# Warm-up matmuls of TensorE in 32x32 tiles of 512 columns, in place of 128x128

## The chip, the cores and the metric

The kernel runs on one core of a Trainium2 chip. The metric is the device time of one execution in microseconds (us). The kernel before the change takes 1802.02 us (median of 3 runs, 1801.92 to 1802.12).

## The reference

The reference mixes two blocks over the same 2048 tokens of 1024 features, with a gate per token. Cut to what matters:

```python
def _A_ref(x, wqkv, wo):                       # attention, 32 heads of 32
    qkv = (x @ wqkv) ...                       # (1024 x 3072) projection
    scores = einsum("bhqd,bhkd->bhqk", q, k) * Dh ** -0.5
    p = softmax(scores); o = einsum("bhqk,bhkd->bhqd", p, v)
    return o @ wo
def _B_ref(x, w_q, k1, k2, u, v):              # 32 routers, each picks 1 of 64 experts
    q = einsum("nd,dhc->nhc", x, w_q); s1 = q1 . k1; s2 = q2 . k2
    e = argmax(s1) * 8 + argmax(s2)
    return sum over h of gelu(x . u[e]) * v[e]
g = sigmoid((x * gate_w).sum(-1, keepdims=True))
return g * a + (1 - g) * b
```

Nothing that the change touches enters this result: the matmuls it replaces write to PSUM banks which the projection then starts anew.

## The kernel before

One function, `gated_mha_peer_kernel`, records every instruction by hand: the schedule is manual, each engine runs its instructions in the order in which the program writes them down, and semaphores join the engines where one needs what another made. There is no planner. So the place of a statement in the source sets its place in its engine's queue, behind everything written for that engine before it.

The projection to Q and K runs in float32 by halves: `split(hi, lo, src)` (L99 to L101) has ScalarE copy `src` to a rounded half `hi` (L100) and VectorE subtract it to give the rest `lo` (L101); a product is then three matmuls (hi.hi, hi.lo, lo.hi). The tokens are cut in four blocks of 512 columns, the 1024 features in eight chunks of 128 (`kc`).

The change lies in the first 30 us of the program, which run as follows.

- Constants: VectorE writes `ones` and an identity matrix `ident` of 128x128 (L96, from an iota of GpSimd).
- Loads of the first weights (`wraw`, by the queues of ScalarE and SyncE) and of the tokens (`xh`, `xl` places, by SyncE) are issued chunk by chunk.
- Splits of the first chunk are written down before any matmul: `split_w0(0, 1)` for the weights of chunk 0, `split_x(0)` for its tokens (two blocks), and then already `split_w0(1, 2)`, the weights of chunk 1. Their halves go to tiles `e` and `xh`.
- Four PSUM banks `b0` are taken (banks 0 to 3), and the warm-up matmuls follow: nine times `ident` by `ident` into the last of the banks (L391). They read nothing but `ident`.
- `mm0` (L395) is the first real product: weights of Q and K chunk 0, two token blocks, eight chunks `kc`, three matmuls each: 96 matmuls of 512 columns into the four banks. The first of each bank starts the bank anew (`start=True`). The splits of chunks 1 to 7 are written between them, chunk by chunk.
- The next product is a plain loop over the same tokens (L491), with the router's folds (`fold`, L311: four matmuls of 32 output columns each, one per quarter of the array) in between. Then come six rounds of a Strassen product (`product`, L155), plain chunks again (L711), the routers (L758, L926), V (L155), attention (`ring` L1292, `o` L1313) and the output projection (`pa`).

The tile pool `ev` with three buffers a name holds the tiles `hi` and `lo` in which the results of the projection are put (`evac_hi`, L240, and `evac_lo`, L253).

The lines around the change:

```python
    split_w0(0, 1)
    split_x(0)
    load_w0(4, KC, nc.sync)
    dma(kraw, k12.rearrange("p (a e) -> p a e", a=2))
    split_w0(1, 2)
...
    b0 = {(w, n): bank() for w in range(2) for n in (2, 3)}
    for i in range(9):                                                             # L390
        nc.tensor.matmul(b0[1, 3][:, :128], ident, ident, start=True, stop=True)   # L391
    def mm0(w, n, kc, i):
        a, b = ((0, 0), (0, 1), (1, 0))[i]
        nc.tensor.matmul(b0[w, n], w_parts[w, kc // HC][:, a, kc % HC], x_at(b, n, kc),
                         start=(kc == 0 and i == 0), stop=(kc == KC - 1 and i == 2))
```

Of the kernel before, what the change touches and what calls it, by code (L numbers as in the profile page):

```python
# [10 lines left out]
F32 = mybir.dt.float32  # L11
# [21 lines left out]
def gated_mha_peer_kernel(ctx, tc, xT, wqkv, wv, wo, wq, k12, ug, v, out):  # L33
# [8 lines left out]
    nc = tc.nc  # L42
# [22 lines left out]
    ident = const.tile([128, 128], F32, name="ident")  # L65
# [128 lines left out]
    def bank():  # L194
        while bank_no[0] % 8 in held:
            bank_no[0] += 1
        i = bank_no[0] % 8
        bank_no[0] += 1
        return ps1.tile([128, 512], F32, name=f"bk{i}")
# [6 lines left out]
    ev = Pool("ev", bufs=3)  # L206
# [180 lines left out]
    b0 = {(w, n): bank() for w in range(2) for n in (2, 3)}  # L387


    for i in range(9):  # L390
        nc.tensor.matmul(b0[1, 3][:, :128], ident, ident, start=True, stop=True)  # L391

    def mm0(w, n, kc, i):
        a, b = ((0, 0), (0, 1), (1, 0))[i]
# [90 lines left out]
    for w in range(2):  # L485
        for n in (2, 3):
            ps = bank()
# [216 lines left out]
    for blk, (k, n) in enumerate(order):  # L704
        w, c = chunks[k]
        t = pairs[k % 2]
        ps = bank()
# [1126 lines left out]
```

## Time and profile before

| | before |
|---|---|
| median of 3 runs | 1802.02 us |
| profiled execution, its own time | 1801.88 us |
| span of its instructions | 1800.1 us |
| TensorE busy (PE) | 1793.7 us, 100% |
| VectorE (DVE), ScalarE (ACT) | 1502.7 us (83%), 1216.7 us (68%) |
| first warm-up matmul, first `mm0` matmul, first L491 matmul | 1.52, 6.14, 30.23 us |

A busy share is the share of the span in which an engine had an instruction under way. PE is the matmul side of TensorE, PEld its weight loads, which overlap. A matmul's record runs longer than its slot, as matmuls are pipelined: the distance from one start to the next is what it costs. A float32 matmul leaves two records, so the nine of the warm-up show as 18, and the four of a fold as 8; a matmul on halves (fp32r) leaves one. The PEclk of the profile is the clock that a throttle granted; it is 1.00 throughout.

### The profile page before, as it was taken

The numbers are of one execution on the slowest core, as the hardware profiler recorded it, in microseconds if no ns is written. First come the engines' busy times: TensorE is split into PE (matmuls) and PEld (weight loads), VectorE is DVE, ScalarE is ACT, GpSimd is POOL, SyncE is SP. The second block draws the span as 40 slices with busy tenths as digits, with TensorE's granted clock in tenths as the row PEclk, the third lists the DMA queues.
The fourth block names the chain that finished last, engine by engine and source line by source line (L and its number), as shares of the span: only waits on it lengthen the run. The fifth ranks groups of instructions, "written<-read, shape, count | busy, mean of one in ns | idle before, by whom it ended". The sixth has DMA issues, their size and how long they took to land.

```text
span 1800.1 us, 27993 instructions
## 1 busy us (share of the span) xinstructions
PE 1793.7 (100%) x10559; PEld 1135.3 (63%) x10559; DVE 1502.7 (83%) x1685; ACT 1216.7 (68%) x1604; POOL 284.0 (16%) x353
## 2 busy tenths in 40 slices
PE   9999999999999999999999999999999999999999
PEld 7877777788888845555455554555554555547887
DVE  7868776358887779899899899999989989897774
ACT  4434321211333399999999999999999999993221
POOL 0222000026401201111111121121111121222000
PEclk9999999999999999999999999999999999999999
DMA  6788889823238688899899999898999999986761
GB/s 239 240 285 252 271 265 289 270 80 107 83 115 281 231 199 176 173 188 194 181 203 200 200 197 192 190 199 190 203 211 206 203 219 190 201 176 216 233 172 59
DMA packets 130454, 359.15 MB, mean 200 GB/s; under 512 B 18648, under 2 KB 56648, under 8 KB 104764
## 3 DMA queue, kind: packets, MB, share of 16 engines
q0 software_dynamic: 22352, 132.98, 36.3%
q1 hardware_dynamic: 87804, 188.42, 36.0%
q10 hardware_dynamic: 20160, 35.92, 7.0%
q8 instruction: 84, 1.38, 0.3%
q14 instruction: 54, 0.44, 0.1%
HBM read 173.72 MB, written 86.61 MB: 145 GB/s over the span
## 4 chain that ended last, share of the span: by engine, by line
PE 98%; DMA 1%; ACT 0%; SPq 0%; issue 0%; DVE 0%; ACTq 0%; DVEq 0%
PE ring L1292 28%; PE o L1313 26%; PE bk L155 13%; PE bk L711 10%; PE pa L155 6%; PE bk L758 5%; PE pa L1571 2%; PE bk L926 2%; PE bk L311 2%; PE bk L491 1%; PE pa L1578 1%; PE bk L395 1%; DMA wraw<-in_wqkv 1%; ACT P L1301 0%; SPq L82 0%; PE o L1326 0%
## 5 line engine op out<-in xcount | busy, mean ns | idle before, releaser
L1301 ACT ACTIVATE P<-ring 128x512 f32<-128x512 f32 (+3 forms) x986 | 808.1, 942 | 14.0 <-PE ring L1292 8.6
L1353 DVE TENSOR_TENSOR acc<-acc,P 128x1024 f32<-128x1024 f32 x408 | 469.7, 1219 | 22.1 <-ACT P L1301 22.1
L1313 PE MATMUL o<-P,V 128*32 128x512 f32 (+1 forms) x4040 | 412.6, 529 | 0.0
L1292 PE MATMUL ring<-Q,K 98*128 98x512 f32 x1024 | 268.7, 406 | 0.1
L1292 PE MATMUL ring<-z,z 98*128 98x512 f32 x1020 | 267.5, 406 | 0.1
L1292 PEld LDWEIGHTS ring<-Q,K 98*128 98x128 f32 x1024 | 182.6, 188 | 116.9 <-ACT P L1301 38.8
L1292 PEld LDWEIGHTS ring<-z,z 98*128 98x128 f32 x1020 | 182.1, 188 | 114.6 <-issue 37.8
L1313 PEld LDWEIGHTS o<-P,V 128*32 128x32 f32 x4040 | 111.5, 109 | 218.3 <-issue 198.6
L1353 DVE TENSOR_TENSOR rb<-rb,P 128x1024 f32<-128x1024 f32 x186 | 214.4, 1219 | 5.6 <-ACT P L1301 5.6
L1342 POOL DMA_DIRECT2D P<-P x60 | 55.7, 928 | 354.6 <-PE o L1313 141.1
L240 ACT ACTIVATE hi<-bk 128x512 fp32r<-128x512 f32 x40 | 23.7, 595 | 117.8 <-PE bk L711 98.7
L1301 ACT ACTIVATE wo_raw<-ring 128x512 f32<-128x512 f32 (+3 forms) x115 | 97.6, 942 | 0.6
L711 PE MATMUL bk<-xh,e 128*128 128x512 f32 x384 | 94.2, 394 | 0.0
L711 PE MATMUL bk<-xl,e 128*128 128x512 f32 x384 | 92.2, 389 | 0.0
L253 DVE TENSOR_TENSOR lo<-bk,hi 128x512 fp32r<-128x512 f32 x40 | 27.6, 690 | 68.8 <-ACT hi L240 66.5
L711 PEld LDWEIGHTS bk<-xh,e 128*128 128x128 f32 x384 | 71.0, 188 | 22.0 <-issue 3.4
L711 PEld LDWEIGHTS bk<-xl,e 128*128 128x128 f32 x384 | 72.1, 188 | 15.0
L101 DVE TENSOR_TENSOR e<-wraw,e 128x512 fp32r<-128x512 f32 (+3 forms) x64 | 55.1, 868 | 27.8 <-ACT e L100 27.3
L1301 ACT ACTIVATE vhl<-ring 128x512 f32<-128x512 f32 (+3 forms) x89 | 76.9, 940 | 0.9 <-PE ring L1292 0.2
L1353 DVE TENSOR_TENSOR acc<-acc,wo_raw 128x1024 f32<-128x1024 f32 x60 | 70.2, 1219 | 1.8 <-ACT wo_raw L1301 1.8
L100 ACT ACTIVATE e<-wraw 128x512 fp32r<-128x512 f32 (+3 forms) x64 | 44.6, 705 | 36.8 <-DMA wraw<-in_wqkv 16.2
L1361 POOL DMA_DIRECT2D acc<-acc x41 | 33.7, 822 | 221.0 <-DMA acc<-acc 83.3
(308 smaller groups left out, 2494.7 us busy)
## 6 DMA issues: line engine op xcount, KB each, us to landing
P<-P POOLq DMA_DIRECT2D x60, 1024.0 KB, 10.3
wqt<-in_wq SPq DMA_DIRECT2D x26, 1024.0 KB
wraw<-in_wqkv SPq DMA_DIRECT2D x30, 512.0 KB
acc<-acc POOLq DMA_DIRECT2D x21, 512.0 KB, 6.3
qdh<-hi ACTq DMA_DIRECT2D x32, 256.0 KB
qdl<-lo ACTq DMA_DIRECT2D x32, 256.0 KB
kdh<-hi ACTq DMA_DIRECT2D x32, 256.0 KB
kdl<-lo ACTq DMA_DIRECT2D x32, 256.0 KB
```

Source lines behind the costliest of these rows:

```text
L100: nc.scalar.activation(hi, src, AF.Copy)
L101: (on or nc.vector).tensor_tensor(out=lo, in0=src, in1=hi.bitcast(F32), op=OP.subtract)
L155: nc.tensor.matmul(ps, self.a[a][i][:, k, :], self.b[b][j][k], start=(not first and k == 0 and i == j == 0), stop=(k == HC - 1 and i == 1))
L311: nc.tensor.matmul(ps[32 * quad:32 * quad + 32, :], kpad[:, quad % 2, i, :], t[:, quad, :], start=(i == 0), stop=(i == 3))
L711: nc.tensor.matmul(ps, t[:, kc // HC, a, kc % HC], x_at(b, n, kc), start=first, stop=last)
L758: nc.tensor.matmul(ps, x_at(a, t // 4, kc)[:, tok], b, start=first, stop=last)
L926: nc.tensor.matmul(p, x_at(a, t // 4, kc)[:, tok], b, start=first, stop=last)
L1292: on_ring(nc.tensor.matmul(ring[:, i, :], K[:98, kt * 128:(kt + 1) * 128], Q[:98, qc * 512:(qc + 1) * 512], start=True, stop=True), i)
L1301: on_ring(nc.scalar.activation(P[h, kt][:, q0 * 512:(q0 + m) * 512].rearrange("p (a m) -> p a m", a=m), ring[:, i:i + m, :], AF.Exp, scale ...
L1313: nc.tensor.matmul(O[h][32 * qc:32 * qc + 32, c0:c1], Vt[g][:, kt, 32 * j:32 * j + 32], p[:, qc * 512 + c0:qc * 512 + c1], start=(kt == 0) ...
L1342: nc.gpsimd.dma_start(P[h, b], P[h, a], accum_op=OP.add)
L1353: nc.vector.tensor_add(out[:, c], a[:, c], b[:, c])
```

## The change

The nine 128x128 matmuls go. In their place a tile `warm` of 128x512 is taken from the pool `ev` (the first buffer of the name `hi`), VectorE sets it to zero, and TensorE runs 32 matmuls of 32x32 stationary values by 512 columns: for each of the four column quarters `c` of the array, one on each of the four row quarters `r`, each row quarter with a bank of its own; and all sixteen twice.

```diff
-    for i in range(9):
-        nc.tensor.matmul(b0[1, 3][:, :128], ident, ident, start=True, stop=True)
+    warm = ev.tile([128, 512], F32, name="hi")
+    nc.vector.memset(warm, 0.0)
+    for i in range(2):
+        for c in range(4):
+            for r, ps in enumerate(b0.values()):
+                rows = slice(32 * r, 32 * r + 32)
+                nc.tensor.matmul(ps[32 * c:32 * c + 32, :], ident[rows, 32 * c:32 * c + 32], warm[rows, :],
+                                 start=True, stop=True)
```

The order of VectorE's queue around the new memset, as a difference of the two programs. The names `e_149` and `e_160` are the weight halves of Q and K, `xh_171` and `xh_173` the token halves of the two blocks; the first two rows are chunk 1 of the weights, the last two chunk 1 of the tokens.

```order
 L101 TENSOR_TENSOR e_149<-wraw_175,e_149 128x128
 L101 TENSOR_TENSOR e_160<-wraw_177,e_160 128x128
+L391 MEMSET hi 128x512
 L101 TENSOR_TENSOR xh_171<-xh_169,xh_171 128x512
 L101 TENSOR_TENSOR xh_173<-xh_169,xh_173 128x512
```

The memset stands behind the splits of the weights of chunk 1 and ahead of the token splits of chunk 1; nothing else on VectorE changes place.

The head of TensorE's queue before, with the engines on which a row waits (`DVE_49` is VectorE, `Activation_49` is ScalarE):

```order
L391 MATMUL bk_219<-ident 128x128 [waits DVE_49]
L391 MATMUL bk_219<-ident 128x128 x8
L395 MATMUL bk_216<-xh_171,e_149 128x512 [waits Activation_49]
L395 MATMUL bk_216<-xh_171,e_149 128x512 [waits DVE_49]
L395 MATMUL bk_216<-xh_171,e_149 128x512
```

The first row waits for `ident`; `mm0` follows the ninth warm-up matmul. The same place now, the first four of the 32 and the first row of `mm0` (now L401):

```order
L396 MATMUL bk_216<-hi,ident 32x512 [waits DVE_49]
L396 MATMUL bk_217<-hi,ident 32x512
L396 MATMUL bk_218<-hi,ident 32x512
L396 MATMUL bk_219<-hi,ident 32x512
...
L401 MATMUL bk_216<-xh_171,e_149 128x512 [waits Activation_49]
```

The first row now reads `hi`, the tile of the memset, so its wait for VectorE is a wait for the memset's place in the queue shown above; all of `mm0` stands behind the 32.

## The prediction

> **What bounds the kernel now.** I read the page first: the span, the busy times, the chain of work that ended last.
>
> ```profile
> span 1800.1 us, 27993 instructions
> PE 98%; DMA 1%; ACT 0%; SPq 0%; issue 0%; DVE 0%; ACTq 0%; DVEq 0%
> ```
>
> The chain is TensorE's own work for 98% of the span: whatever shifts that work shifts the end, unless TensorE waits somewhere later for something that does not shift with it. So I asked for the windows by stage and for TensorE's waits (engine, line waited for, total us, times, longest) of the stretch from 17.2 to 640 us.
>
> ```profile
> 0.00:30.00 30.00, 27.78 (x114) 21.79 (x114) 19.59 (x41) 16.73 (x29) 0.43 (x5) 1.00 0.78 281
> 30.00:180.00 150.00, 150.00 (x710) 115.86 (x709) 117.80 (x150) 57.09 (x89) 30.11 (x23) 1.00 0.80 249
> 380.00:480.00 100.00, 99.61 (x441) 81.63 (x440) 80.80 (x161) 12.37 (x25) 58.76 (x64) 1.00 0.19 61
> 1000.00:1590.00 590.00, 590.00 (x4121) 297.58 (x4114) 547.71 (x491) 581.56 (x731) 98.85 (x124) 1.00 0.95 199
> PE bk L758 <- ACT xu L762: 0.4, 1, 0.4
> ```
>
> The first figure behind the length of a window is PE's busy time. It is full from 30 us on, but for 0.4 us at the routers, and that one wait is for ScalarE, which itself waits there for a matmul. Only the first 30 us hold idle time, 2.2 us. That is where the change lies, so the question is when TensorE gets through the work of these 30 us. The chain there, and the timeline of the two engines:
>
> ```profile
> 17.17 13.21 PE bk L395 x57
> 30.39 5.44 PE bk L491 x24
> ...
> 0.88 0.11 DVE L72 MEMSET ones<- 128x64 f32 x1
> 1.26 0.20 DVE L96 TENSOR_SCALAR ident<-jp 128x128 f32<-128x128 int32 x1
> 1.52 4.21 PE L391 MATMUL bk<-ident 128*128 128x128 f32 x18 [1.52 <-DVE ident L96]
> 6.14 13.37 PE L395 MATMUL bk<-xh,e 128*128 128x512 f32 x48 [0.41 <-ACT xh L100]
> 9.06 0.29 DVE L101 TENSOR_TENSOR e<-wraw,e 128x128 fp32r<-128x128 f32 x1 [1.19 <-ACT e L100]
> 9.58 1.29 DVE L101 TENSOR_TENSOR xh<-xh,xh 128x512 fp32r<-128x512 f32 x2 [0.23 <-ACT xh L100]
> 13.36 0.69 DVE L101 TENSOR_TENSOR e<-wraw,e 128x512 fp32r<-128x512 f32 x1 [0.61 <-ACT e L100]
> 18.32 0.27 DVE L285 MEMSET kpad<- 128x256 f32 x1
> 19.34 11.04 PE L395 MATMUL bk<-xl,e 128*128 128x512 f32 x48
> 30.23 2.88 PE L491 MATMUL bk<-xh,e 128*128 128x512 f32 x12
> ```
>
> The warm-up fills the wait for the first data: it starts at 1.52, as soon as `ident` is there, and is over before the first `mm0` matmul can run at 6.14. The first 48 matmuls of `mm0` take 13.2 us because their chunks arrive late; the second 48 run without a stop, (30.23 - 19.34) / 48 = 0.2269 us each. Up to 17.17 the chain comes from loads and splits, after it TensorE never waits again.
>
> **The change part by part.** *The memset.* It is new on VectorE and stands behind the split of chunk 1's weights, the row at 9.06, which waits for a load by way of ScalarE. So it cannot start before 9.06 + 0.29 = 9.35. Its length by the two memset rows: 64 elements take 0.11 and 256 take 0.27, so 512 take about 0.27 + 256 x 0.16 / 192 = 0.48. It ends at 9.83. `ident` was done at 1.46 and its reader began at 1.52, a hand-over of 0.06; so the warm-up starts at **9.89**, not 1.52. Behind the memset on VectorE stand the token splits of chunk 1, which ran at 9.58 and now run about 0.25 later; all that follows is late by that much until the row at 13.36, ahead of which VectorE was idle for 0.61. So the delay is gone at 13.36. Who waits for those splits is `mm0` of chunk 1, which by the sum below does not start before 16 us: cost nothing.
>
> *The nine matmuls removed.* They ended before `mm0` could run and were hidden by the wait for data: their removal gains nothing.
>
> *The 32 matmuls added.* All of `mm0` is behind them in TensorE's queue. Their price depends on two things that the trace does not show for this form: how many 32x32 tiles run side by side, and at which clock. Rows for both:
>
> ```profile
> L391 PE MATMUL bk<-ident x18: 421/421/582, 1.5 to 5.3; 128*128 128x128 f32 x18
> L395 PE MATMUL bk<-xh,e x48: 387/393/651, 6.1 to 19.1; 128*128 128x512 f32 x48
> 89.88:90.34 0.46, 0.45 (x4) 0.16 (x8) 1.00 0.00 0
> 90.34:90.77 0.43, 0.43 (x8) 0.13 (x4) 1.00 0.00 0
> 90.77:91.20 0.43, 0.43 (x8) 0.13 (x4) 1.00 0.00 0
> 35.76 1.06 PE L311 MATMUL bk<-wqt,kpad 128*32 128x512 f32 x8
> 36.75 3.02 PE L491 MATMUL bk<-xh,e 128*128 128x512 f32 x12
> ```
>
> The three windows are a fold: four float32 matmuls of 512 columns on four column quarters start together, one new set of four records every 0.43 us (the count in a window includes the four still running). So quarters do run side by side, and the two records of a matmul are two sets. The warm-up's 18 records of 128 columns are 3.8 / 17 = 0.22 us apart, which is 0.89 for 512 columns: twice 0.43. TensorE ran at half speed there, although the granted clock reads 1.00 in both. If all sixteen tiles run side by side, the 32 matmuls are 2 x 2 = 4 sets; at half speed 4 x 0.86 to 0.89 = 3.4 to 3.6, I take **3.5**. Bounds: at full speed throughout 4 x 0.43 = 1.7; with nothing side by side 64 records in a row, 64 x 0.43 = 27.5 and more. I take four sets because the quarters of the fold behave so, with rows and columns alike separate quarters here, and half speed because TensorE has been idle before, as it had at 1.52.
>
> [...] No row here has more than four side by side.
>
> *`mm0` behind it.* Going back from 32-column tiles to the full array costs: two sets from 35.76 end at 36.62, and L491 follows at 36.75, 0.13. So `mm0` starts at 9.89 + 3.5 + 0.13 = **13.52**. Its 96 matmuls then take 96 x 0.2269 = 21.78, plus 0.14 for the restart (12 matmuls at 36.75 take 3.02, those at 30.23 take 2.88). Nothing stops it: by 13.52 the splits of chunks 0 to 2 are nearly through; the last splits of chunk 3 end at about 15.83 + 1.29 = 17.12 by the row below, and `mm0` needs them at 13.52 + 36 x 0.2269 = 21.7.
>
> ```profile
> 15.83 1.29 DVE L101 TENSOR_TENSOR xh<-xh,xh 128x512 fp32r<-128x512 f32 x2
> ```
>
> *The clock.* Before, TensorE was still slow at 5.3, 3.8 us after its warm-up began, and the 651 ns of the longest `mm0` record (its first, at 6.14, to 6.79) look slow too; then records fall to about 390. So it became fast 3.8 to 5.3 us after the start. From 9.89 that is 13.7 to 15.2: `mm0` runs slow for its first 0.2 to 1.7 us and loses half of it, 0.1 to 0.85. I take 0.5.
>
> [...]
>
> *Sum.* L491 starts at 13.52 + 21.78 + 0.14 + 0.5 = 35.94 against 30.23: **5.7 us later**. Taking `warm` from the pool of `hi` costs nothing: its readers end at 13.4, and the buffer is wanted again by the third evacuation, after 35 us. The evacuations themselves wait for `mm0` and move with it. On the profiled execution of 1801.88 (span 1800.1) the sum gives 1807.6; the median of the runs lies 0.14 above it, so I forecast **1807.7**. With its own bounds (3.4 to 3.6, and 0.1 to 0.85) the case runs from 1807.2 to 1808.2.
>
> **The rivals.** *Nine sets (15%).* Tiles run side by side only in the fours in which they are issued, and the second records of a four start together with the first of the next: 8 + 1 = 9 sets. Five at half speed (up to 4.4 us), four at full: 4.4 + 1.7 = 6.1, and `mm0` starts at 16.1, fast. L491 at 38.0, 7.8 late: 1809.8; if the clock rises late, up to 1 us more. For it: only fours are seen in the trace. [...]
>
> *Sixteen sets (8%).* Fours side by side and no overlap between fours: 5 x 0.89 + 11 x 0.43 = 9.2, `mm0` at 19.2, L491 at 41.1, 10.9 late: 1812.9. *Nothing side by side (4%).* 64 records, 5 of them slow: 4.4 + 59 x 0.43 = 29.8, 31.5 late: 1833.5.
>
> *It does not warm (8%).* The sixteen tiles run as foreseen, but small tiles do not count as work for the clock: `mm0` then runs slow for 3.8 to 5.3 us and loses 1.9 to 2.7 instead of 0.5. That is 7.1 to 7.9 late, 1809.1 to 1809.9. Against it: the tiles fill the array.
>
> *Fast from the start (4%).* The clock is up during the warm-up: 1.7 instead of 3.5, no loss behind it, 3.4 late: 1805.4. Against it the warm-up of before, slow for all its 3.8 us.
>
> *The other side: paid back at the end of attention (6%).* There the chain leaves TensorE:
>
> ```profile
> 1592.18 2.49 SPq L82
> 1596.72 3.39 DMA vhl<-vpl
> 1603.54 0.50 PE ring L1292
> ```
>
> If SyncE's loads at 1592 are held by something that does not start with TensorE, they stay where they are, and 2.49 + 3.39 = 5.9 us of waiting swallow the 5.7: 1801.9, no change, or a little faster. It decides whether the issue at 1592.18 moves with `mm0`. Against it: the step ahead of it in the chain is ScalarE's work on attention's results, which moves. For the lateness not to arise at all, `mm0` would have to start by 30.23 - 21.78 - 0.14 = 8.31, ahead of the memset's 9.35: the order excludes it.
>
> **How the numbers follow.** Forecast 55%, nine sets 15%, sixteen 8%, none 4%, no warming 8%, fast 4%, paid back 6%. About 0.2% or 3.6 us is what a measurement here can tell from no change. Slower by more: 55 + 15 + 8 + 4 + 8 = 90%; the fast case (3.4 us) and most of the paid-back one are within, 8%; faster 2%. The range goes from the fast case, 1805.4, to the sixteen sets at 1812.9; outside are the paid-back case, no overlap, and the slow half of sixteen sets, some 14%.
>
> **What would show it.** The first 32x32 row near 9.9 us and ended by VectorE's memset; its 64 records in four sets 0.86 apart, over by 13.5; the first `mm0` record at 13.5, its first few 0.43 apart and the rest 0.227 with no wait; L491 at 35.9; each later stage 5.7 later, attention's end too. A first 32x32 row near 1.6, more than four sets, or a late stage that starts at its old time makes it wrong.

## The result, and the profile after

The changed kernel takes 1807.97 us (median of 6 runs, 1807.77 to 1808.34) against 1802.07 for the kernel before beside it (6 runs): 5.9 us or 0.33% slower, ratio 1.0033, 95% interval 1.0023 to 1.0043. The forecast was 1807.7. Its profiled execution took 1808.07 us, its span is 1806.3.

The chain of work that ended last, at its head (start, length, what; all in us):

```profile
2.16 6.53 DMA wraw<-in_wqkv
8.69 0.02 issue
8.71 0.32 ACT e L100
9.03 0.02 issue
9.06 0.04 DVE e L101
9.09 0.31 issue
9.40 0.50 DVE hi L391
9.90 0.04 issue
9.94 4.08 PE bk L396 x64
14.03 22.62 PE bk L401 x96
36.65 5.44 PE bk L497 x24
```

This is the change in one view. The second load of chunk 1's weights lands at 8.7, ScalarE and VectorE split it, then VectorE runs the memset, and only then do the small matmuls start; `mm0`, the first product with data, follows them. Before, the loads reached the chain by way of the splits that `mm0` itself needed; now they reach it by way of a tile of zeros. The timeline, first rows of VectorE, then those of TensorE, answers to the one of before:

```profile
9.40 0.48 DVE L391 MEMSET hi<- 128x512 f32 x1
9.81 1.22 DVE L101 TENSOR_TENSOR xh<-xh,xh 128x512 fp32r<-128x512 f32 x2
...
14.69 1.29 DVE L101 TENSOR_TENSOR e<-wraw,e 128x512 fp32r<-128x512 f32 x2 [1.79 <-ACT e L100]
9.94 4.08 PE L396 MATMUL bk<-hi,ident 32*32 32x512 f32 x64 [9.94 <-DVE hi L391]
13.96 11.81 PE L401 MATMUL bk<-xh,e 128*128 128x512 f32 x48
25.61 11.04 PE L401 MATMUL bk<-xl,e 128*128 128x512 f32 x48
36.49 2.88 PE L497 MATMUL bk<-xh,e 128*128 128x512 f32 x12
```

L401 is L395 of before, L497 is L491: 36.49 against 30.23, 6.26 later, and the span is 6.2 longer. From 19.34 us of the old trace on, no matmul moved by more than 0.15 us against this shift. Behind its first row TensorE again waits only at the routers:

```profile
PE bk L764 <- ACT xu L768: 0.3, 1, 0.3
```

The windows of the small matmuls alone (length; PE busy and its records; weight loads and their records; granted clock; DMA share; GB/s; a count holds the records still running):

```profile
9.94:10.79 0.85, 0.85 (x16) 0.29 (x32) 1.00 0.66 215
10.79:11.64 0.85, 0.85 (x32) 0.17 (x1) 1.00 0.85 225
11.64:12.50 0.86, 0.86 (x32) 0.58 (x31) 1.00 1.13 184
12.50:13.96 1.46, 1.46 (x32) 0.00 (x0) 1.00 0.74 238
```

Sixteen records start at once, one per tile, a new set every 0.85 us: four sets, at half speed (a fold's set of 512 columns took 0.43). In the third window the weights of the second round are loaded while its matmuls should run.

### The profile page after: what moved, and what is told of

Read it like the earlier page. It is cut to its first block, busy times and chain, and to the rows that moved or that the text cites. A ratio compares the mean times of both kernels' runs of the same rounds, so it can differ in the third digit from the quotient of the medians.

```text
span 1806.3 us, 28086 instructions
## 1 busy us (share of the span) xinstructions
PE 1792.2 (99%) x10605; PEld 1132.9 (63%) x10605; DVE 1503.4 (83%) x1686; ACT 1216.9 (67%) x1604; POOL 284.0 (16%) x353
## 4 chain that ended last, share of the span: by engine, by line
PE 98%; DMA 1%; ACT 0%; SPq 0%; issue 0%; ACTq 0%; DVE 0%; DVEq 0%
PE ring L1298 28%; PE o L1319 26%; PE bk L155 13%; PE bk L717 10%; PE pa L155 6%; PE bk L764 5%; PE pa L1577 2%; PE bk L932 2%; PE bk L311 2%; PE bk L401 1%; PE bk L497 1%; PE pa L1584 1%; ACT P L1307 0%; DMA wraw<-in_wqkv 0%; DMA vhl<-vpl 0%; PE o L1332 0%
## 5 line engine op out<-in xcount | busy, mean ns | idle before, releaser
L717 PE MATMUL bk<-xh,e 128*128 128x512 f32 x384 | 94.2, 394 | 0.0
L155 PE MATMUL bk<-xh,e 128*128 128x512 f32 x288 | 68.5, 393 | 0.0
```

The costliest lines, as they stand in the source:

```text
L155: nc.tensor.matmul(ps, self.a[a][i][:, k, :], self.b[b][j][k], start=(not first and k == 0 and i == j == 0), stop=(k == HC - 1 and i == 1))
L717: nc.tensor.matmul(ps, t[:, kc // HC, a, kc % HC], x_at(b, n, kc), start=first, stop=last)
```

## The experiments

Two theories of the 5.9 us. **A, the place:** the memset stands behind work that waits for loads, the warm-up waits for the memset, and `mm0` for the warm-up; the form of the matmuls is harmless. **B, the form:** the small tiles cost, by their length, by the change back to the full array, or by not raising the clock. All edits are to the changed kernel.

**The memset early.**

```diff
+    warm = ev.tile([128, 512], F32, name="hi")
+    nc.vector.memset(warm, 0.0)
     split_w0(0, 1)
...
-    warm = ev.tile([128, 512], F32, name="hi")
-    nc.vector.memset(warm, 0.0)
     for i in range(2):
```

> The memset is written ahead of the first splits, so it is the first thing on VectorE after the identity; the 32 small matmuls stay as they are. Theory A (the place of the memset in VectorE's queue holds the warm-up, and all of the projection behind it): memset from 1.5 to 1.9 us, small matmuls 2.0 to 6.0, first real matmul at 6.1 to 6.3, L491's counterpart at 30.2 to 30.6, median 1801.9 to 1802.5. Theory B (the small-tile form itself costs, by its length, its mode change or a clock it does not raise): most of the 5.9 us stays, median 1804.5 or more.

Measured: 1801.64 us against 1801.78 before, ratio 1.0000 (0.9991 to 1.0009). The timeline:

```profile
1.52 0.48 DVE L376 MEMSET hi<- 128x512 f32 x1
2.06 4.09 PE L396 MATMUL bk<-hi,ident 32*32 32x512 f32 x64 [2.06 <-DVE hi L376]
6.25 12.75 PE L401 MATMUL bk<-xh,e 128*128 128x512 f32 x48
29.71 2.88 PE L497 MATMUL bk<-xh,e 128*128 128x512 f32 x12
```

The same 32 matmuls, as long as in the changed kernel, now fit into the wait for the first data. The whole loss is gone; theory B cannot say that.

**The memset on another engine.**

```diff
-    nc.vector.memset(warm, 0.0)
+    nc.gpsimd.memset(warm, 0.0)
```

> The memset stays where it is written but goes to GpSimd, whose queue holds only the iota ahead of it. Theory A: it ends by about 2 us, the small matmuls run from 2 to 6.1, and the median is that of the kernel before within 0.5 us: 1801.7 to 1802.6. Theory B: as for the early memset, 1804.5 or more.

Measured: 1801.79, ratio 0.9999 (0.9990 to 1.0008). One word, at the place in the source where the change has it: GpSimd's queue is empty behind the iota, and the row reads

```profile
1.04 0.52 POOL L391 MEMSET hi<- 128x512 f32 x1
```

so the memset was over at 1.56, and the small matmuls started at 1.78, when `ident` (over at 1.63) was there too. It was the queue, not the statement.

**The old matmuls, late.**

```diff
-    for i in range(2):
-        ...
+    for i in range(9):
+        nc.tensor.matmul(b0[1, 3][:, :128], ident, warm[:, :128], start=True, stop=True)
```

> The nine matmuls of 128x128 by 128 columns of before, but with the zeroed tile as moving operand, so that they wait for the memset where the change put it. Theory A: they start at 9.9, take 3.8 us at half speed, the first real matmul is at 13.9, and the median is that of the changed kernel, 1807.5 to 1808.2. Theory B (the form costs): clearly below it, 1805 or less.

Measured: 1807.66, ratio 1.0034 (1.0021 to 1.0046). The 128x128 form, made to wait for the same memset, costs the same:

```profile
9.93 4.11 PE L393 MATMUL bk<-hi,ident 128*128 128x128 f32 x18 [9.93 <-DVE hi L391]
13.79 11.15 PE L397 MATMUL bk<-xh,e 128*128 128x512 f32 x48
35.66 2.88 PE L493 MATMUL bk<-xh,e 128*128 128x512 f32 x12
```

L493 starts 5.43 late here; another 0.42 went near 123.6 us, for a cause that the trace does not name. With the two runs above, this settles it: form and place were exchanged one at a time, and the time goes with the place.

**The memset halfway,** behind the first token splits and ahead of `split_w0(1, 2)`.

```diff
     dma(kraw, k12.rearrange("p (a e) -> p a e", a=2))
+    warm = ev.tile([128, 512], F32, name="hi")
+    nc.vector.memset(warm, 0.0)
     split_w0(1, 2)
```

> The memset between the place of the first experiment and that of the change: behind the first token splits and ahead of the split of chunk 1's weights, which ended at 7.4 to 7.8 us. Theory A: the small matmuls start at 7.9 to 8.3, 1.6 to 2.0 us ahead of the changed kernel's, and the end follows one for one: median 1805.9 to 1806.4. Theory B: no change against the changed kernel, 1807.9.

Measured: 1805.78 (1805.08 to 1807.11), ratio 1.0023 (1.0014 to 1.0032), just under the range that A gave. The small matmuls started at 8.11, 1.83 ahead of the changed kernel's, and the median is 2.2 lower; against the kernel before beside each of the two, it is 4.0 late in place of 5.9, 1.9 less. In the profiled execution L497 starts at 34.94, only 1.55 ahead, since here more of `mm0` ran at half speed (below).

**No warm-up.**

```diff
-    warm = ev.tile([128, 512], F32, name="hi")
-    nc.vector.memset(warm, 0.0)
-    for i in range(2):
-        ...
```

> No warm-up at all. Theory A says that what the warm-up buys is small, because the first matmuls wait for loads anyway: the real matmuls start at 6.1 at half speed, 0.43 us apart, for 4 to 5.3 us, which loses 2 to 2.6 us of work, and the waits of before for chunks 1 and 3 (about 2 us up to 17.2) take most of it back: 0 to 0.8 us late, 1802.0 to 1802.9. Rival C (the warm-up is needed): the full loss stays, 1804.0 to 1804.7.

Measured: 1802.14 (1801.49 to 1802.66), ratio 1.0002 (0.9993 to 1.0011). Rival C is out: this kernel has next to nothing to win by a warm-up. The timeline, and what TensorE's weight loads waited for up to 30 us:

```profile
6.22 13.99 PE L393 MATMUL bk<-xh,e 128*128 128x512 f32 x48 [6.22 <-ACT xh L100]
...
PEld bk L393 <- ACT xh L100: 6.2, 1, 6.2
PEld bk L393 <- DVE xh L101: 0.4, 1, 0.4
```

After the 6.2 us up to its first data TensorE waits 0.4 us more. In the kernel before the weight loads of `mm0` waited, behind the warm-up, for the two engines that split:

```profile
PEld bk L395 <- ACT xh L100: 1.9, 5, 0.7
PEld bk L395 <- DVE xh L101: 1.3, 3, 0.4
```

The slow clock makes `mm0` late (its first 48 matmuls take 13.99 us, against 13.37 in the kernel before), and a late `mm0` finds its data ready: the loss sits where a fast clock would have waited.

**One round in place of two,** late as the change has it, run twice.

```diff
-    for i in range(2):
+    for i in range(1):
```

> The late warm-up cut to one round: 16 small matmuls in place of 32, memset where the change put it. Theory A with a clock that rises a set time after work begins (in the changed kernel about 5.2 us after 9.94): small matmuls from 9.94 to 11.7, first real matmul at 12.0, at half speed until about 15.2, so of the 2.0 us won about 1.0 is lost again: median 1806.8 to 1807.2. Rival D (the clock rises after a set number of matmuls or columns, or not from small tiles): if small tiles do not count, the first real matmuls are slow for 4 us or more, to 16 or later, and the median is 1807.4 or more. Rival E (clock plays no part): the whole 2.0 us is won, 1805.9.

Measured: 1808.38 (1807.73 to 1809.87), ratio 1.0039 (1.0025 to 1.0052). None of A, D and E foresaw the trace whole. Its head went as A said:

```profile
9.86 2.02 PE L396 MATMUL bk<-hi,ident 32*32 32x512 f32 x32 [9.86 <-DVE hi L391]
11.81 12.28 PE L401 MATMUL bk<-xh,e 128*128 128x512 f32 x48
34.81 2.88 PE L497 MATMUL bk<-xh,e 128*128 128x512 f32 x12
```

L497 is 1.68 ahead of the changed kernel's. But near 537 us TensorE waited, which it did in no other trace so far:

```profile
PE bk L155 <- DVE xh L161: 0.4, 1, 0.4
PE bk L155 <- DVE xh L101: 0.4, 1, 0.4
```

and behind this stood a load of V's tokens for which ScalarE waited, issued at 521.35 and taken up 8.4 us later:

```profile
521.35 0.39 SPq L82 DMA_DIRECT2D xl<-in_xT  x1
529.78 0.63 ACT L100 ACTIVATE a<-xl 128x512 fp32r<-128x512 f32 x1 [4.37 <-DMA xl<-in_xT]
```

In the changed kernel the same load was issued at 523.02 and taken up at 530.01, 7.0 later. To see whether that was chance, the kernel ran again, beside the changed kernel.

> The late warm-up cut to one round, a second time. In its first trace the first 36 us went as theory A says (first real matmul at 11.8, fast from about 14.1, L491's counterpart at 34.8, which is 1.7 us ahead of the changed kernel), but 1.3 us were lost again near 537 us, where TensorE waited for a load of V's tokens. Theory F (that stop is a chance of one execution, as loads differ between executions): it is not there, or not at the same place, in this trace, and the median is 1806.3 to 1807.8, below the changed kernel beside it. Theory G (this version stops there always): the stop is there again and the median is again 1808 or more.

> The changed kernel once more, on the same chip as the one-round version, so that the two can be compared. The clock rose 5.3 us after the start of the warm-up in its first trace and between 3.9 and 6.0 us in those of the other versions: if that moment varies between executions, it is another here, and the median lies between 1807.3 and 1808.5.

Measured: 1808.28 (1807.2 to 1808.79), ratio 1.0035 (1.0023 to 1.0047), for one round; 1807.69 (1807.17 to 1808.3), ratio 1.0032 (1.0020 to 1.0044), for the changed kernel. Theory F fails: the stop was there again, shorter (the load took 8.0 us, from then on all was some 0.9 us later), so G stands as far as two traces go. The issue follows L497's shift in all traces, so the load itself is slower: 8.4 and 8.0 us here, 6.5 to 7.1 in the other eight. It ends with sixteen packets of 4 bytes. In all ten traces fifteen of them are through 6.7 us after the issue; the last ends at 6.2 to 6.7 us in the eight, at 7.9 and 7.5 in these two. And these two alone have, in the 6.5 us after the issue, a packet of the DMA queue that loads instructions:

```profile
q8 instruction: 1, 0.02, 1.4%
q8 instruction: 1, 0.02, 1.2%
```

It is 16 KB long and ran from 5.5 to 7.0 and from 5.3 to 6.5 us after the issue. So the likely cause is that in the shorter program this load of instructions falls into the load of V's tokens and holds up its last part. No run moves that packet alone, so this is not shown. The rest of the 2 us went to the clock. The first 48 of `mm0` take 11.04 us when nothing holds them and the clock is up, as the second 48 show. With the warm-up late they have no data to wait for, so what lies above 11.04 is the clock's, but for some 0.1 of the restart. The second traces of one round and of the changed kernel:

```profile
10.03 2.02 PE L396 MATMUL bk<-hi,ident 32*32 32x512 f32 x32 [10.03 <-DVE hi L391]
11.97 12.91 PE L401 MATMUL bk<-xh,e 128*128 128x512 f32 x48
```

```profile
9.98 4.08 PE L396 MATMUL bk<-hi,ident 32*32 32x512 f32 x64 [9.98 <-DVE hi L391]
13.99 11.51 PE L401 MATMUL bk<-xh,e 128*128 128x512 f32 x48
```

One round lost 1.24 and 1.87 us that way, two rounds 0.77 and 0.47, the halfway memset (12.10) 1.06, the old form late (11.15) 0.11. So in these two pairs of traces the shorter warm-up gave back much of what it saved: `mm0` started 2.0 to 2.1 us sooner, and the clock took 0.5 to 1.4 more.

## Why the prediction was right

Step by step, as it was put:

- *The memset starts at 9.35, takes 0.48, and the warm-up starts at 9.89.* Measured 9.40, 0.48 and 9.94. The step that decided the case, the place in VectorE's queue read from the order and the time of the row ahead of it read from the trace, was right to 0.05 us.
- *The delay on VectorE costs nothing.* The token splits moved from 9.58 to 9.81, and VectorE was idle again, for 1.79 us, ahead of its row at 14.69. TensorE never waited for it.
- *The nine matmuls removed gain nothing.* Shown by the run without any warm-up, which is no faster.
- *Four sets, half speed, 3.5, and 0.13 to go back: 3.63.* Four sets and half speed are in the windows above, so the nine and sixteen sets, the serial case and the fast clock from the start are out. From first small matmul to `mm0` it took 4.02: this term was 0.4 too small. The loads show where: the first two sets have their 32 weight loads in the first window, while all but one of the second round's come only in the third. There the second record starts 0.24 after the first (11.89 and 11.65), and the sixteen then follow less closely (second to last start from 11.89 to 12.12, in the set before from 10.81 to 10.91). One round, which has no such reload, took 11.81 - 9.86 = 1.95, against 2 x 0.85 + 0.13 = 1.83 by the same reckoning. So the second round cost 4.02 - 1.95 = 2.07 where two sets are 1.70: most of the 0.4 is the reload.
- *No row here has more than four side by side.* In the changed kernel sixteen ran so. Two records a matmul did not stop the tiles from running side by side: the first window of 0.85 us holds sixteen, all of one set.
- *`mm0` takes 21.78 + 0.14 + 0.5 for the clock.* From 13.96 to 36.49 it took 22.53, against 22.42. The clock term, by the rows above, was between 0.4 and 0.7 in two executions. It rose 1.4 and 0.8 us after `mm0` began, against 5.7 where `mm0` was the first work. So small tiles do raise the clock: the case of no warming is out.
- *5.7 later, carried to the end.* 6.26 at L497 and 6.2 at the end in the profiled execution, 5.9 by the medians. The 0.55 between 5.71 and 6.26 is 0.05 of the start, the 0.4 of the sets and 0.1 of `mm0`. That the median came within 0.3 of the forecast is in part luck: the profiled execution of before lay 0.2 under its median, that of the changed kernel 0.1 above, and the moment at which the clock rises moves a single execution by some tenths (L497 at 36.49 and 36.23 in two).
- *Not paid back.* The place where that rival would have shown is the end of attention:

```profile
1598.33 0.89 SPq L82
...
1600.79 5.28 DMA vhl<-vpl
...
1609.68 0.50 PE ring L1298
```

SyncE's issue of 1592.18 is at 1598.33, 6.15 later, and TensorE is back at 1609.68 against 1603.54, 6.14 later. The loads moved with the work ahead of them.

## What to carry to other kernels

Work that is put in front of an engine's queue to fill a wait is only free if its own inputs are there before the wait ends: look at what stands ahead of the producer in the producer's queue, not at how long the producer takes. Here a 0.48 us memset, written a few lines too late, cost 5.9 us, and moving it, or giving it to an idle engine, took all of it back. Before polishing a warm-up, leave it out once: where the first matmuls wait for loads anyway, a slow clock can hide in those waits, as it did here: 1802.14 us without any warm-up, against 1801.78 with it.

## What the runs showed of the hardware

The clock rose at moments that differ between executions of the same program. The rows show it (512 columns every 0.43 us before, every 0.23 after), and each trace keeps records of the granted clock with the moment itself. It rose 5.4 and 4.8 us after the first small matmul in the two traces of the changed kernel, 4.3 and 5.6 in those of one round, 6.0 with the halfway memset, 4.4 with the early one and 3.6 with GpSimd's; 5.7 without warm-up (counted from `mm0`), 3.9 with the old form late, and 5.0 in the kernel before.

The granted clock in the profile's rows nevertheless reads 1.00 through all of this. The reason is that the trace's clock records begin only with the first rise, at 15.31 us in the changed kernel; the time ahead of it has no record and counts as full speed. Where there is a record, behind the last matmul of the kernel before, the row shows half speed (0.50, the figure behind the five engines):

```profile
1798.60:1800.10 1.50, 0.00 (x0) 0.00 (x0) 0.00 (x0) 0.00 (x0) 0.00 (x0) 0.50 0.03 9
```

By the same records the stretch at full clock lasts 1791.997 us both in the kernel before, from 6.49 us on, and in the changed kernel, from 15.31. What sets the moment of the rise no run shows; in all ten traces it lies 3.6 to 6.0 us after the first matmul.

Not foreseen was the reload: the weights of a second round over the same sixteen tiles were loaded only as its matmuls were due (31 of 32 loads in the window from 11.64), and that round took 2.07 us in place of 1.70.
